# Where source order begins, two sums and a sign on GpSimd, and values one slot earlier, in a single-core attention and feed-forward kernel

## The chip, the cores and the metric

The kernel runs on one core of a Trainium2 chip. A core has TensorE (PE, matmuls, with its weight loads shown as PEld), VectorE (DVE), ScalarE (ACT), GpSimd (POOL) and a queue that issues DMAs (SP). Each engine works through its own instructions in a fixed order and waits on semaphores for the others. The metric is the device time of one execution in microseconds. Three runs of the kernel before gave 858.89, 858.98 and 859.55 us, a median of 858.98. The profile is of one further execution, which took 860.12 us; its span from the first to the last instruction is 858.2 us.

## The reference

Attention in chunks of 64 tokens, without any link between chunks, then a feed-forward layer with a gate:

```python
scores = scale * np.matmul(q_c, k_c.transpose(0, 1, 2, 4, 3))
scores = scores - np.max(scores, axis=-1, keepdims=True)
attn = np.exp(scores)
attn = attn / (np.sum(attn, axis=-1, keepdims=True) + 1e-09)
out = np.matmul(attn, v_c)
...
h = x @ w_in
relu6 = np.clip(h + 3.0, 0.0, 6.0)
g = h * relu6 / 6.0
return (g @ w_out).astype(np.float32)
```

q, k and v have the shape (8, 8, 576, 64) in float32. x has 4608 tokens of 512 values, w_in is 512 x 2048 and w_out 2048 x 512. The reference makes the weights in float64, and the kernel gets them as pairs of 32-bit words.

## The kernel before

The 4608 tokens are nine blocks of 512. Every product of the feed-forward layer is made of three TensorE passes (`passes`, lines 219 to 223): each float32 operand is split into a high part and a low part in TensorE's format fp32r, and high x high, high x low and low x high are summed. So for each operand there is a copy that rounds (on ScalarE) and a subtraction that gives the rest (on VectorE).

The first three blocks take the plain way, and this case is about them. The 2048 hidden values are 16 f tiles of 128. For one f tile of one block, `mm1` (225) makes h with 12 matmuls of 512 columns, L233 and L234 apply the gate, L235 rounds g and L236 subtracts for g's low half. `mm2` (242) adds the f tile to the four accumulators (`acc`, `ps_o`) with 12 more matmuls. It runs two f tiles behind `mm1` (`LAG` = 2). The blocks come in four segments: block 0 f tiles 0 to 3, block 1 all 16, block 0 f tiles 4 to 15, block 2 all 16 (line 29). Block 0's first four f tiles are put away as `part` and added when its second segment ends (L259). The last six blocks go through a scheme with fewer multiplications (lines 471 to 630), which needs sums and differences of quarters of the weights in DRAM.

A slot is one `mm1` or one `mm2`. Slots are counted over the four segments: block 1 begins with slot 8, so its f tile k has the slots 8 + 2k and 9 + 2k; there are 96. `plan` holds side work for each slot, run after the slot's matmuls are written (line 443). `finish` (215) then writes the subtractions that were put into `low`, L236 among them.

Three kinds of side work matter here:

- Conversions (`convert`, 100 to 116). A weight tile of 128 x 1024 float64 values arrives as words; ScalarE scales the high word (L106), VectorE shifts the result by three bits (L107) and puts the sign bit of the high word on it (L108), adds the low word that ScalarE scaled (L110, L111), and the result is split (L115, L116). There are 16 tiles. The scratch pool `wsc` holds u and r twice each, at the right end of SBUF. The first four tiles are converted in the opening and block 0's first segment, the other twelve in block 1.
- Attention (`Attention`, 128 to 209), a piece of a block at a time: scores (64 small matmuls into two PSUM banks, `ps_a`), softmax in four steps on VectorE and ScalarE, eight transposes into the same two banks, a copy back to SBUF on ScalarE (L185), values (64 small matmuls into the same banks), a copy out (L200, or L203 with L206). `ps_a` has one buffer, so each step waits until the one before it has left the banks. The list `later` (401) puts the steps of six attentions at slots relative to 30, 38, 52, 60, 68 and 76.
- Sums of the weights (`prepare`, 325 to 353), sixteen of them in three steps each: three DMAs of w and two sums of the low and high part (L334), then four sums and differences (L344) and a rounding copy to `hl` (L347), then a subtraction (L349) and four DMAs of hl. `a` and `hl` have one buffer each. They lie in the pool `sp`, which is opened where `wsc` was.

Up to slot `SUMS` the order on each engine is made by the language's planner, from its own costs; `issue_after` holds VectorE's conversions of tiles 4 and later behind block 1's attention. At slot `SUMS` (20, block 1's f tile 6) the scratch pool is closed, `sp` and `op` are opened, and `manual_schedule` sets source order for everything that follows (436 to 441). The sums are spread from `SUMS` to two slots before `FREE` (86), a start every four slots.

Of the kernel before, what the change touches and what calls it, by code (L numbers as in the profile page):

```python
# [8 lines left out]
F32 = mybir.dt.float32  # L9
F32R = mybir.dt.float32r  # L10
BF16 = mybir.dt.bfloat16
I32 = mybir.dt.int32
U32 = mybir.dt.uint32
AF = mybir.ActivationFunctionType
ALU = mybir.AluOpType
AX = mybir.AxisListType

P = 128
# [7 lines left out]
NCT, NFT, NET = DM // P, DFF // P, DO // P  # L26
# [15 lines left out]
def tile_kernel(ctx: ExitStack, tc: tile.TileContext, qk_in, v_in, weights, out):  # L42
    nc = tc.nc
    PE, ACT, DVE, POOL = nc.tensor, nc.scalar, nc.vector, nc.gpsimd
# [17 lines left out]
    op = None  # L62
# [29 lines left out]
    def load_to(ft):  # L92
        nonlocal loaded
        while loaded < min(ft, NFT):
            t = w_tile(loaded, I32).rearrange("p l m t -> p (l m t)")
            nc.sync.dma_start(out=t.rearrange("p (m t) -> p m t", m=2), in_=weights[loaded].bitcast(I32).rearrange("m p t -> p m t"))
            words[loaded] = t.rearrange("p (n t) -> p n t", t=2)
            loaded += 1

    def convert(ft):  # L100

        u = wsc.tile([P, 1024], I32, name="u")
        r = wsc.tile([P, 1024], I32, name="r")
        lo, hi = words[ft][:, :, 0], words[ft][:, :, 1]

        ACT.activation(out=u.bitcast(F32), in_=hi.bitcast(F32), func=AF.Copy, scale=2.0 ** -112)  # L106
        DVE.tensor_scalar(out=u, in0=u, scalar1=3, scalar2=None, op0=ALU.logical_shift_left)  # L107
        DVE.scalar_tensor_tensor(out=u, in0=hi, scalar=-2 ** 31, in1=u, op0=ALU.bitwise_and, op1=ALU.bitwise_or)  # L108

        ACT.activation(out=r, in_=lo.bitcast(U32), func=AF.Copy, scale=2.0 ** -29)  # L110
        DVE.tensor_tensor(out=u, in0=u, in1=r, op=ALU.add)  # L111
        a = u.bitcast(F32).rearrange("p (m t) -> p m t", m=2)
        w[ft] = w_tile(ft, F32R)
        w_h[ft], w_l[ft] = w[ft][:, 0], w[ft][:, 1]
        ACT.copy(out=w_h[ft], in_=a)  # L115
        DVE.tensor_tensor(out=w_l[ft], in0=a, in1=w_h[ft].bitcast(F32), op=ALU.subtract)  # L116

    def convert_to(ft):
        nonlocal converted
        load_to(ft + 3)  # L120
        while converted < min(ft, NFT):
            convert(converted)
            converted += 1
# [91 lines left out]
    def finish():  # L215
        while low:
            low.pop(0)()

    def passes(ps, a_h, a_l, b_h, b_l, first, last, more=False):

        PE.matmul(ps, lhsT=a_h, rhs=b_h, start=first, stop=False, skip_group_check=more)  # L221
        PE.matmul(ps, lhsT=a_h, rhs=b_l, start=False, stop=False, skip_group_check=more)  # L222
        PE.matmul(ps, lhsT=a_l, rhs=b_h, start=False, stop=last, skip_group_check=more)  # L223
# [15 lines left out]
    acc = []  # L239
    part = {}  # L240

    def mm2(n, ft, g, first, last, spill):

        if first:
            acc[:] = [ps_o.tile([P, NT], F32, name="acc") for et in range(NET)]
        for et in range(NET):
            o = slice(et * P, (et + 1) * P)
            passes(acc[et], w_h[ft][:, 1, o], w_l[ft][:, 1, o], g[:, 0, :], g[:, 1, :], first, last)
            if last:
                before = part.get((n, et))  # L250
                if spill:
                    t = keep.tile([P, NT], F32, name=f"part{n}_{et}")
                elif op:
                    t = op.tile([P, NT], F32, name="o")
                else:
                    o2 = o2 if et % 2 else gp.tile([P, 2, NT], F32, name="g")
                    t = o2[:, et % 2]
                if before is not None:
                    DVE.tensor_tensor(out=t, in0=acc[et], in1=before, op=ALU.add)  # L259
                elif et % 2:  # L260
                    DVE.tensor_copy(out=t, in_=acc[et])
                else:
                    ACT.copy(out=t, in_=acc[et])
                if spill:
                    part[n, et] = t
                else:
                    nc.sync.dma_start(out=out[o, n * NT:(n + 1) * NT], in_=t)
# [16 lines left out]
    keep = rpool("keep", 1)  # L284
    scratch = ExitStack()
    wsc = scratch.enter_context(tc.tile_pool(name="wsc", bufs=2, side="right"))

    with tc.tile_pool(name="ps_b", bufs=2, space=bass.MemoryType.PSUM) as ps_b:
        both = [Attention(0, dp, lambda: two_banks(ps_b)) for dp in range(NDP)]
# [35 lines left out]
    def prepare(m, p):  # L325
        cols = lambda k: slice(256 * k, 256 * k + 256)
        for i, row, col in ((1, 0, 0), (2, 0, 1), (4, 1, 1)):
            f, k = quarter(m, row, col)
            to = kept(m, p, i).rearrange("p (l t) -> p l t", l=2)
            nc.sync.dma_start(out=to, in_=w[p + NFP * f][:, :, m, cols(k)].bitcast(F32))  # L330
        a = sp.tile([P, 2, 512], F32, name="a")
        for f in range(2):
            h, l = [w[p + NFP * f][:, k, m].bitcast(F32) for k in range(2)]
            DVE.tensor_tensor(out=a[:, f], in0=h, in1=l, op=ALU.add)  # L334
        yield

        def q(row, col):
            f, k = quarter(m, row, col)
            return a[:, f, cols(k)]


        for to, x, y, op in ((q(1, 1), q(1, 0), q(1, 1), ALU.add), (q(1, 0), q(0, 0), q(1, 0), ALU.subtract),
                             (q(0, 0), q(1, 1), q(0, 0), ALU.subtract), (q(0, 1), q(0, 1), q(0, 0), ALU.subtract)):
            DVE.tensor_tensor(out=to, in0=x, in1=y, op=op)  # L344
        hl = sp.tile([P, 2, 2, 2, 256], F32R, name="hl")
        s = a.rearrange("p f (k t) -> p f k t", k=2)
        ACT.copy(out=hl[:, :, :, 0], in_=s)  # L347
        yield
        DVE.tensor_tensor(out=hl[:, :, :, 1], in0=s, in1=hl[:, :, :, 0].bitcast(F32), op=ALU.subtract)  # L349
        for i, row, col in ((5, 1, 1), (7, 1, 0), (6, 0, 0), (3, 0, 1)):  # L350
            f, k = quarter(m, row, col)
            nc.sync.dma_start(out=kept(m, p, i), in_=hl[:, f, k].rearrange("p l t -> p (l t)").bitcast(F32))
        yield
# [23 lines left out]
    def x_operands(s, eng):  # L377
# [6 lines left out]
        for i in ORDER_A:  # L384
# [6 lines left out]
            elif i == 6:  # L391
# [7 lines left out]
    plan = {}  # L399
    early = [(0, "load_qk"), (1, "load_v"), (2, "scores"), (2, "softmax"), (7, "transpose"), (10, "values")]  # L400
    later = [(-2, "load_qk"), (3, "load_v"), (3, "scores"), (4, "soft", 0), (4, "soft", 1), (5, "soft", 2), (5, "soft", 3),
             (8, "transpose"), (10, "values")]

    def put(n, dp, at, steps, stretch=1.0):
        a = Attention(n, dp)
# [4 lines left out]
    put(1, 0, -2, early, 0.45)  # L410
    second = put(1, 1, 3, early, 0.45)
    first = [2 * sum(hi - lo for _, lo, hi in SEGMENTS[:i]) for i in range(len(SEGMENTS) + 1)]
    SUMS = first[1] + 12
    FREE = first[3] + 2 * (NFP + LAG + 1)
    for (n, dp), at in zip(((2, 0), (2, 1), (3, 0), (4, 0), (4, 1), (3, 1)), (30, 38, 52, 60, 68, 76)):
        put(n, dp, at, later)
    for u in range(2 * NFP):
        for k in range(3):
            plan.setdefault(SUMS + u * (FREE - 2 - SUMS) // (2 * NFP) + k, []).append((20, lambda: next(prep)))
    prep = (step for p in range(NFP) for m in range(2) for step in prepare(m, p))  # L420
# [4 lines left out]
    for i, (n, lo, hi) in enumerate(SEGMENTS):  # L425
        last = all(m != n for m, *_ in SEGMENTS[i + 1:])
        for ft in range(lo, hi):
            if i == 0:
                convert_to(min(ft + 2, 4))
            elif slot < SUMS:  # L430

                with tc.issue_after(second.done.ins):
                    convert_to(5)
                with tc.issue_after(second.last.ins):
                    convert_to(6 + 2 * ft)
            elif slot == SUMS:
                scratch.close()
                sums = ExitStack()
                sp = sums.enter_context(tc.tile_pool(name="sp", bufs=1, side="right"))
                op = sums.enter_context(tc.tile_pool(name="op", bufs=4, side="right"))  # L440
                order.enter_context(tc.manual_schedule())
            for _ in moe_slots(n, ft, ft == lo, ft == hi - 1, not last):
                for _, f in sorted(plan.pop(slot, []), key=lambda s: s[0]):
                    f()
                finish()
                slot += 1
                if slot == FREE:
                    assert next(prep, None) is None
                    sums.close()
                    op = None  # L450
                    start.close()
                    upper.close()
                    xop_pool = pool("xop", 8, side="right")
                    wsp = pool("wsp", 3, side="right")
                    for _ in range(3):
                        fetch()
                    made = x_operands(0, DVE)
                elif slot > FREE:
                    next(made, None)

    for item in pending:
        mm2(*item)
# [4 lines left out]
    op = pool("op2", 2)  # L467
# [189 lines left out]
```

## Time and profile before

| what | value |
|---|---|
| median of three runs | 858.98 us |
| the profiled execution | 860.12 us |
| its span | 858.2 us |
| mean granted TensorE clock | 0.974 |
| TensorE busy with matmuls | 813.4 us (95%) |
| VectorE busy | 636.2 us (74%) |
| ScalarE busy | 367.4 us (43%) |
| GpSimd busy | 128.9 us (15%) |

TensorE is busy in nearly all of the span, so time is lost where it stands idle or runs at a lower clock. The page shows the span in 40 equal slices of 21.5 us; the digits are the busy share in tenths:

```profile
PE   6988929999998999999999999999999999999998
PEld 4766818878876878878878888788788887887886
DVE  6978996776767667487699956876999466669951
ACT  4747744244243335334356442344554433336330
POOL 0000000000000000021318003212270022335200
PEclk9798969999998999999999999999999999999999
```

PE's line has a 2 in the sixth slice (107 to 129 us), where the clock also falls to 0.6, while DVE's line has a 9 there. The thirteenth slice (257 to 279 us) has an 8. The first two slices are the opening: loads, the first attention, the first conversions. GpSimd does next to nothing before the eighteenth slice.

A row of the timeline has the start, the duration, the engine, the line, the operation, the written and read names with their shapes, and in brackets the idle time of the engine before it with what ended that. A row of the list of waits has the waiting instruction, what it waited for, the total, the number of times and the longest.

### The profile page before, as it was taken

What the parts mean: (1) busy time and instruction counts of PE and PEld (TensorE: products, weight loads), DVE (VectorE), ACT (ScalarE), POOL (GpSimd) and SP (SyncE); (2) the same over time, 40 slices, a digit from 0 to 9 for tenths busy, and PEclk for the clock granted to TensorE, in tenths of its full rate; (3) what the DMA queues carried; (4) which work ended last, traced back from release to release, by engine and by line L of the source; (5) the groups of instructions that cost most, each with busy time, mean ns of one, the idle gap of its engine ahead of it and who ended that gap; (6) DMA issues with size and microseconds to landing.
All of it is one profiled execution on the core that took longest, in us unless ns stands there. A gap on an engine that the chain in (4) does not pass through costs nothing.

```text
span 858.2 us, 13692 instructions
## 1 busy us (share of the span) xinstructions
PE 813.4 (95%) x5683; PEld 659.2 (77%) x5683; DVE 636.2 (74%) x770; ACT 367.4 (43%) x453; POOL 128.9 (15%) x75
## 2 busy tenths in 40 slices
PE   6988929999998999999999999999999999999998
PEld 4766818878876878878878888788788887887886
DVE  6978996776767667487699956876999466669951
ACT  4747744244243335334356442344554433336330
POOL 0000000000000000021318003212270022335200
PEclk9798969999998999999999999999999999999999
DMA  9791006767664565156555676666555765555564
GB/s 365 298 375 67 13 0 215 218 203 249 208 207 174 175 231 210 49 222 238 204 191 215 244 224 232 227 238 224 199 194 183 223 228 187 193 200 196 196 208 136
DMA packets 50014, 172.86 MB, mean 201 GB/s; under 512 B 4640, under 2 KB 16928, under 8 KB 39200
## 3 DMA queue, kind: packets, MB, share of 16 engines
q1 hardware_dynamic: 49952, 171.99, 57.6%
q8 instruction: 45, 0.74, 0.3%
q14 instruction: 17, 0.14, 0.0%
HBM read 133.17 MB, written 38.80 MB: 200 GB/s over the span
## 4 chain that ended last, share of the span: by engine, by line
PE 64%; DVE 21%; ACT 6%; issue 4%; DMA 3%; SPq 1%; POOL 0%; ACTq 0%; DVEq 0%
PE acc L221 14%; PE acc L222 13%; PE acc L223 13%; PE h L221 6%; PE h L222 6%; PE h L223 6%; DVE xop L370 2%; PE two L194 2%; DVE a L344 2%; ACT r L233 2%; DVE r L234 1%; DMA w<-w_in_out 1%; DVE z L168 1%; DVE m L161 1%; PE two L154 1%
## 5 line engine op out<-in xcount | busy, mean ns | idle before, releaser
L221 PE MATMUL acc<-xop,ws 128*128 128x512 f32 x528 | 208.8, 396 | 4.4 <-DVE u L481 4.4
L222 PE MATMUL acc<-xop,ws 128*128 128x512 f32 x528 | 206.0, 390 | 0.0
L223 PE MATMUL acc<-xop,ws 128*128 128x512 f32 x528 | 205.6, 390 | 0.0
L501 POOL TENSOR_TENSOR g<-g 128x512 f32<-128x512 f32 x24 | 34.8, 1448 | 572.0 <-DVE g L493 572.0
L221 PEld LDWEIGHTS acc<-xop,ws 128*128 128x128 f32 x528 | 99.2, 188 | 27.7 <-DVE u L481 6.8
L370 DVE TENSOR_TENSOR xop<-g,xop 128x1024 fp32r<-128x1024 f32 x72 | 103.3, 1466 | 21.5 <-ACT xop L369 21.5
L223 PEld LDWEIGHTS acc<-xop,ws 128*128 128x128 f32 x528 | 99.2, 188 | 20.9
L222 PEld LDWEIGHTS acc<-xop,ws 128*128 128x128 f32 x528 | 99.3, 188 | 19.6
L369 ACT CAST xop<-g 128x1024 fp32r<-128x1024 f32 x72 | 74.4, 1050 | 78.9 <-PE acc L223 51.3
L222 PE MATMUL acc<-g,w 128*128 128x512 f32 x192 | 77.3, 403 | 16.4 <-DVE g L236 16.4
L221 PE MATMUL acc<-g,w 128*128 128x512 f32 x192 | 77.6, 408 | 3.3 <-DVE o L259 3.3
L221 PE MATMUL h<-x,w 128*128 128x512 f32 x192 | 78.3, 410 | 2.3 <-ACT x L203 1.9
L234 DVE SCALAR_TENSOR_TENSOR r<-r,h 128x512 f32<-128x512 f32 x48 | 32.8, 684 | 62.6 <-ACT r L233 62.5
L222 PE MATMUL h<-x,w 128*128 128x512 f32 x192 | 77.6, 405 | 0.0
L223 PE MATMUL acc<-g,w 128*128 128x512 f32 x192 | 77.2, 402 | 0.0
L223 PE MATMUL h<-x,w 128*128 128x512 f32 x192 | 76.9, 401 | 0.0
L492 ACT ACTIVATE r<-acc,half 128x512 f32<-128x512 f32 x72 | 48.5, 685 | 26.3 <-DVE acc L481 25.4
L492 ACT ACTIVATE r<-h,half 128x512 f32<-128x512 f32 x24 | 16.5, 687 | 94.9 <-DVE h L481 94.9
L222 PE MATMUL h<-xop,ws 128*128 128x512 f32 x144 | 56.2, 391 | 0.2 <-DVE xop L370 0.2
L222 PEld LDWEIGHTS acc<-g,w 128*128 128x128 f32 x192 | 37.1, 193 | 25.0 <-DVE g L236 17.2
L221 PE MATMUL h<-xop,ws 128*128 128x512 f32 x144 | 56.4, 391 | 0.0
L223 PE MATMUL h<-xop,ws 128*128 128x512 f32 x144 | 56.2, 390 | 0.0
(91 smaller groups left out, 1275.4 us busy)
## 6 DMA issues: line engine op xcount, KB each, us to landing
ws<-b SPq DMA_DIRECT2D x42, 1024.0 KB, 4.8
ws<-a SPq DMA_DIRECT2D x24, 1024.0 KB, 4.8
ws<-a SPq DMA_DIRECT2D x24, 768.0 KB, 4.3
qk<-qk_in SPq DMA_DIRECT2D x17, 1024.0 KB, 6.5
w<-w_in_out SPq DMA_DIRECT2D x16, 1024.0 KB, 13.2
v<-v_in SPq DMA_DIRECT2D x17, 512.0 KB, 5.4
a<-hl SPq DMA_DIRECT2D x32, 256.0 KB, 3.4
b<-hl SPq DMA_DIRECT2D x32, 256.0 KB, 3.0
```

What stands on the lines that cost most here:

```text
L154: PE.matmul(self.s[o, a, c, :], lhsT=self.qk[rows, 0, c, o], rhs=self.qk[rows, 1, c, o], start=True, stop=True)
L194: PE.matmul(po[o, s, a, i, :], lhsT=self.v[rows, a, i, o], rhs=self.aT[rows, a, i, o], start=True, stop=True)
L221: PE.matmul(ps, lhsT=a_h, rhs=b_h, start=first, stop=False, skip_group_check=more)
L222: PE.matmul(ps, lhsT=a_h, rhs=b_l, start=False, stop=False, skip_group_check=more)
L223: PE.matmul(ps, lhsT=a_l, rhs=b_h, start=False, stop=last, skip_group_check=more)
L233: ACT.activation(out=r, in_=h, func=AF.Relu, bias=half, scale=1.0 / 6.0)
L234: DVE.scalar_tensor_tensor(out=r, in0=r, scalar=1.0, in1=h, op0=ALU.min, op1=ALU.mult)
L344: DVE.tensor_tensor(out=to, in0=x, in1=y, op=op)
L369: ACT.copy(out=t[:, :, 0], in_=src)
L370: DVE.tensor_tensor(out=t[:, :, 1], in0=src, in1=t[:, :, 0].bitcast(F32), op=ALU.subtract)
L492: return (lambda: ACT.activation(out=r, in_=ps, func=AF.Relu, bias=half, scale=1.0 / 6.0), lambda: DVE.scalar_tensor_tensor(out=out, in0=r ...
L501: sub = lambda o, x, y: lambda: POOL.tensor_tensor(out=o, in0=x, in1=y, op=ALU.subtract)
```

## The change

Four things change.

1. `SUMS` goes from `first[1] + 12` (slot 20, f tile 6 of block 1) to `first[1] + 22` (slot 30, f tile 11). The planner makes the order of ten slots more, the scratch pool is closed ten slots later, and the sixteen sums start every three or four slots from slot 30 to slot 80. `min(6 + 2 * ft, NFT)` keeps the number of tiles asked for at 16.
2. In block 0's final sums (four parts, `et` 0 to 3) the odd two are made by a copy on ScalarE and an addition in SBUF on GpSimd, where VectorE made them from PSUM.
3. In `later`, values stand one slot behind the transposes, where they stood two behind.
4. In a conversion, GpSimd multiplies the high word, read as a float32, by zero, which leaves a zero with the word's sign. VectorE then shifts by three and joins the sign in one instruction, where it had two. The sign tile has its own pool with one buffer.

```diff
@@ -104,8 +104,10 @@
         ACT.activation(out=u.bitcast(F32), in_=hi.bitcast(F32), func=AF.Copy, scale=2.0 ** -112)
-        DVE.tensor_scalar(out=u, in0=u, scalar1=3, scalar2=None, op0=ALU.logical_shift_left)
-        DVE.scalar_tensor_tensor(out=u, in0=hi, scalar=-2 ** 31, in1=u, op0=ALU.bitwise_and, op1=ALU.bitwise_or)
+
+        sign = sgn.tile([P, 1024], F32, name="sign")
+        POOL.tensor_scalar(out=sign, in0=hi.bitcast(F32), scalar1=0.0, scalar2=None, op0=ALU.mult)
+        DVE.scalar_tensor_tensor(out=u, in0=u, scalar=3, in1=sign.bitcast(I32), op0=ALU.logical_shift_left, op1=ALU.bitwise_or)
@@ -255,7 +257,10 @@
-                if before is not None:
+                if before is not None and et % 2:
+                    ACT.copy(out=t, in_=acc[et])
+                    POOL.tensor_tensor(out=t, in0=t, in1=before, op=ALU.add)
+                elif before is not None:
                     DVE.tensor_tensor(out=t, in0=acc[et], in1=before, op=ALU.add)
@@ -284,6 +289,7 @@
     wsc = scratch.enter_context(tc.tile_pool(name="wsc", bufs=2, side="right"))
+    sgn = scratch.enter_context(tc.tile_pool(name="sgn", bufs=1, side="right"))
@@ -399,7 +405,7 @@
     later = [(-2, "load_qk"), (3, "load_v"), (3, "scores"), (4, "soft", 0), (4, "soft", 1), (5, "soft", 2), (5, "soft", 3),
-             (8, "transpose"), (10, "values")]
+             (8, "transpose"), (9, "values")]
@@ -410,7 +416,7 @@
-    SUMS = first[1] + 12
+    SUMS = first[1] + 22
@@ -432,7 +438,7 @@
                 with tc.issue_after(second.last.ins):
-                    convert_to(6 + 2 * ft)
+                    convert_to(min(6 + 2 * ft, NFT))
```

## The prediction

> **What bounds the kernel now.** I read the busy time by stretches first, then the list of waits, then the timeline of VectorE and TensorE around the longest wait.
>
> ```profile
> 72.00:107.00 35.00, 34.57 (x147) 27.33 (x146) 34.17 (x39) 27.86 (x33) 0.00 (x0) 0.99 0.02 8
> 107.00:127.00 20.00, 3.58 (x17) 2.61 (x15) 18.33 (x20) 10.21 (x11) 0.00 (x0) 0.66 0.00 0
> 127.00:330.00 203.00, 196.49 (x1560) 159.09 (x1560) 139.44 (x219) 74.40 (x100) 0.00 (x0) 0.97 0.64 204
> ...
> PE acc L222 <- DVE g L236: 16.4, 1, 16.4
> ...
> PE acc L221 <- DVE o L259: 3.3, 1, 3.3
> ...
> PE two L194 <- ACT e L185: 2.9, 3, 1.2
> ...
> PE two L154 <- ACT x L200: 2.4, 2, 1.5
> ```
>
> The columns of the first three rows are the stretch, its length, then busy time (and instructions) of PE, weight loads, DVE, ACT and POOL, the granted clock, the DMA share and GB/s. TensorE sets the time nearly everywhere: 34.57 of 35 us and 196.49 of 203 us busy. The exception is the 20 us between them, where it works 3.58 us and VectorE 18.33. That hole is one wait of 16.4 us, for the low half of g that L236 writes. Three small waits follow: for accumulators to be emptied (L259, 3.3 us) and for the two banks that attention reuses (L200, 2.4 us in two waits).
>
> ```profile
> 106.03 1.23 DVE L116 TENSOR_TENSOR w<-u,w 128x1024 fp32r<-128x1024 f32 x1
> ...
> 123.71 1.23 DVE L116 TENSOR_TENSOR w<-u,w 128x1024 fp32r<-128x1024 f32 x1 [1.17 <-ACT w L115]
> 124.97 1.29 DVE L334 TENSOR_TENSOR a<-w 128x512 f32<-128x512 f32 x2
> 126.18 0.68 DVE L236 TENSOR_TENSOR g<-r,g 128x512 fp32r<-128x512 f32 x1
> ...
> 110.11 0.39 PE L221 MATMUL acc<-g,w 128*128 128x512 f32 x1
> 126.92 0.79 PE L222 MATMUL acc<-g,w 128*128 128x512 f32 x1 [16.42 <-DVE g L236]
> ...
> 130.49 0.43 PE L221 MATMUL acc<-g,w 128*128 128x512 f32 x1
> ```
>
> The columns are start, duration and instruction. L334 is the first of the weights' sums. It writes a tile that lies where the conversions' scratch lay, so it cannot start before the sixteenth conversion ends (L116 at 123.71 plus 1.23). From slot 20 on the order is that of the source, so L236 of block 1's seventh f tile stands behind it. The twelfth conversion was at its last step at 106.03, so four were still open when TensorE arrived. The eight matmul starts from 126.92 to 130.49 stand 0.446 us apart (in the first stretch 34.57 us held 147 matmuls, 0.235 each), so the low clock after the hole costs another 1.7 us. The hole is worth 16.4 + 1.7 = 18.1 us.
>
> **The change, part by part.** (1) *Source order from slot 30.* The slots between go back to the planner, ten slots of 12 matmuls, 28 us. One conversion ran per f tile:
>
> ```profile
> 83.51 0.69 DVE L107 TENSOR_SCALAR u<-u 128x1024 int32<-128x1024 int32 x1
> 84.11 0.68 DVE L234 SCALAR_TENSOR_TENSOR r<-r,h 128x512 f32<-128x512 f32 x1
> 84.72 1.23 DVE L116 TENSOR_TENSOR w<-u,w 128x1024 fp32r<-128x1024 f32 x1
> 85.86 1.22 DVE L108 SCALAR_TENSOR_TENSOR u<-w,u 128x1024 int32<-128x1024 int32 x1
> 87.00 0.69 DVE L236 TENSOR_TENSOR g<-r,g 128x512 fp32r<-128x512 f32 x1
> 87.60 1.22 DVE L111 CUSTOM_DVE_ANT_0 u<-u,r 128x2048 uint16<-128x2048 uint16 x1
> 88.74 0.69 DVE L107 TENSOR_SCALAR u<-u 128x1024 int32<-128x1024 int32 x1
> ```
>
> A round takes 88.74 - 83.51 = 5.23 us on VectorE, against 24 x 0.235 = 5.6 us on TensorE. At 5.6 us a round the last four conversions end near 106.0 + 1.2 + 4 x 5.6 = 129.6. L236 of the twelfth f tile, now the first behind L334, is then done at 129.6 + 1.2 + 0.7 = 131.5. TensorE needs it five f tiles after the present hole, at 110.1 + 28 + 0.2 = 138.3. The margin is 6.8 us, so the whole 18.1 us goes, and nothing is late next at that place.
>
> The sixteen sums are the same work, squeezed from 64 slots into 54. VectorE was busy 139.44 of 203 us there; in 28 us less it is 80% busy, still covered by TensorE. A sum now follows the last after 3 or 4 slots instead of 4, and its L347 must wait until the DMAs of the last one have read hl. Such a wait (4.89 us before 147.19, first row below) did not stop TensorE, which was busy 10.00 of those 10 us; its cover is the two f tiles between a gate and its use. Each sum issues seven DMAs on SP's queue, three of w and four of hl. The DMA share goes from 0.64 to some 0.64 x 203 / 175 = 0.74. The loads of q, k and v between them keep their slots, five or more ahead of their use (14 us), so I cost their delay at nothing; POOL's queue is empty there.
>
> ```profile
> 147.19 1.05 ACT L347 CAST hl<-a 128x1024 fp32r<-128x1024 f32 x1 [4.89 <-DMA b<-hl]
> ...
> 140.00:150.00 10.00, 10.00 (x46) 8.29 (x45) 6.21 (x12) 3.23 (x5) 0.00 (x0) 1.00 0.90 272
> ...
> 168.01 0.38 PE L183 MATMUL two<-ident,e 128*128 128x128 f32 x2
> ...
> 174.12 1.01 ACT L185 COPY e<-two 128x1024 f32<-128x1024 f32 x1
> ...
> 238.84 0.62 ACT L235 CAST g<-r 128x512 fp32r<-128x512 f32 x1 [0.76 <-DVE r L234]
> ...
> 241.17 0.62 ACT L235 CAST g<-r 128x512 fp32r<-128x512 f32 x1 [1.12 <-DVE r L234]
> 241.70 1.01 ACT L185 COPY e<-two 128x1024 f32<-128x1024 f32 x1
> ...
> L183 PE MATMUL two<-ident,e x8: 271/272/273, 322.4 to 323.2; 128*128 128x128 f32 x8
> ...
> 327.18 1.01 ACT L185 COPY e<-two 128x1024 f32<-128x1024 f32 x1
> ```
>
> (2) *Values one slot after transposes* instead of two, in six attentions. This adds a wait. Values read what L185 copies, and L185 stands on ScalarE behind L235 of its slot. L235 waits for L234, and L234 waits on VectorE behind sums and softmax (238.84 to 241.70 above). So L185 ends late: 174.12 + 1.01 is 6.1 us after the first attention's eight transposes end (168.01 + 1.04, their time in the next fence). For the six it is 6.1, 5.5, 4.9, 7.1, 4.6 and 4.7 us, the last from 323.5 to 328.2. Before, 24 matmuls (5.6 us) lay between; now 12 do, 2.8 us. What is left over is 3.3 + 2.7 + 2.1 + 4.3 + 1.8 + 1.9 = 16.1 us of TensorE waiting, with all later matmuls queued behind. The first gets some 2 us more (its L347 is one that would stand two slots behind the last sum, with hl still being read); the fourth some 2 less, since it lies behind the L259 rows that (3) thins. They cancel. Before, 0.6 us of this was already there, so 15.5 us is new. In return, values leave the banks a slot sooner, and the two waits for L200 go: 2.4 us.
>
> ```profile
> L263 ACT COPY o<-acc x2: 567/578/589, 188.5 to 189.0; 128x512 f32<-128x512 f32 x2
> ...
> 248.78 1.16 PE L154 MATMUL two<-qk 64*64 64x64 f32 x64 [1.45 <-ACT x L200]
> ...
> 263.81 1.04 PE L183 MATMUL two<-ident,e 128*128 128x128 f32 x8
> 267.32 2.48 DVE L259 TENSOR_TENSOR o<-acc,part 128x512 f32<-128x512 f32 x4
> 268.15 0.77 PE L221 MATMUL acc<-g,w 128*128 128x512 f32 x1 [3.30 <-DVE o L259]
> ...
> 273.83 0.44 PE L222 MATMUL h<-x,w 128*128 128x512 f32 x1
> ```
>
> (3) *Two of block 0's four sums on GpSimd.* ScalarE copies two accumulators (0.58 us each, by the first row) beside two adds on VectorE, and L349, which stood just ahead, falls in another slot. The first accumulator is free some 2.2 us earlier: 3.3 us becomes 1.1. Thirteen matmul steps from 268.15 to 273.83 took 0.437 us instead of 0.235, 2.6 us; after 1.1 us of waiting I expect none of that, since matmuls after the 1.45 us wait for L200 came at full pace. Worth 2.2 + 2.6 = 4.8 us. The GpSimd adds feed only output DMAs.
>
> (4) *Sign on GpSimd.* L107 goes, 0.60 us of each conversion; the new combined step takes L108's place and 1.14 us. VectorE's round falls to 4.63 us. GpSimd gets one instruction of 128x1024 elements, one input, which the trace does not have. Its neighbours:
>
> ```profile
> L381 POOL TENSOR_TENSOR x<-x x8: 2394/2403/2417, 453.8 to 691.6; 128x1024 f32<-128x1024 f32 x8
> ...
> L65 POOL MEMSET r<- x1: 524/524/524, 0.7 to 0.7; 128x512 f32 x1
> ...
> L550 POOL TENSOR_TENSOR g<-g,t x12: 3315/3382/3397, 458.5 to 795.4; 128x1024 f32<-128x1024 f32 x12
> ...
> L548 DVE TENSOR_TENSOR g<-t,g x12: 1208/1218/3429, 386.9 to 793.1; 128x1024 f32<-128x1024 f32 x12
> ```
>
> L548, two SBUF inputs, takes 1.21 us alone and 3.43 beside L550: GpSimd's work is added to VectorE's. So a GpSimd product of length H costs VectorE up to H a round. Twice the memset is 1.05 us, the two-input L381 2.40 us. I take 1.05, the row with one stream. The round is then 5.68 us, 0.08 over TensorE's 5.6; by the source twelve of the sixteen conversions lie in block 1, so 1 us. The ends are 0 (no collision: the round of 4.63 hides under TensorE, which was already full, so nothing is gained) and 12 x (4.63 + 2.40 - 5.6) = 17.2 us. The other four stand in the opening, where one conversion more or less on VectorE can move the first products: between 4 x -0.60 and 4 x (2.40 - 0.60), -2.4 to +7.2 us. I take 0, because the 1.05 and the 0.60 nearly balance and not all of it lies on the path.
>
> A slow clock after the new waits: the first, some 5 us, gets the 2.6 us seen after 3.3 us; the others lie between 1.45 (none) and 3.3 us, and I take 1 us for all.
>
> By the Trainium skill ("TensorE: Matmul & The Clock Gate", Part 1) the clock halves after an idle window of about 3.4 us. Here 3.30 us was enough. By the page alone that 1 us would be 0, and the sum 1 us better.
>
> **The sum.** Gains 18.1 + 4.8 + 2.4 = 25.3; losses 15.5 + 2.6 + 1 + 1 = 20.1; net -5.2 us. The profiled execution took 860.1 us (span 858.2), 1.1 above the median of 858.98. Both ends of my sum lie inside the span, so I subtract from the median: **853.8 us**.
>
> **Rivals.** *A, the forecast:* hole gone, values late; 848 to 857.3 with the sizes of the waits, clock and copies. *B, values are not late:* if less softmax and sum work stands ahead of L185 in the new order, it ends within 2.8 us, and between a third and most of the 19.1 us that A loses to late values falls away (6 to 17 us): 837 to 848. For it: the sums' steps fall in other slots than before. Against: even the best of the six was 4.6 us, of which L233, L234, L235 and L185 in a row need 2.9. *C, GpSimd blocks VectorE:* at H = 2.40 the conversions cost 12 x 1.35 = 16.2 us more than in A, L334 again starts late and TensorE waits at the new boundary: 853.8 + 16.2 = 870.0, slower than before. It decides from H = 1.05 + 5.2/12 = 1.5 us. For it: L548 beside L550. Against: one input, not two.
>
> The Trainium skill ("SBUF — State Buffer", SBUF: two separate sides) says that a VectorE instruction with two SBUF inputs and a GpSimd instruction exclude each other for the whole instruction. The 3.43 us of L548 agrees; it speaks for C. "GPSIMD Engine Reference", Engine selection, calls one-input work roughly line-rate, which speaks for A's 1.05; no run here shows it yet.
>
> That the hole stays because the planner again leaves conversions to the boundary is part of C: the same wait, the same signs.
>
> **Chances.** A 0.57, B 0.24, C 0.19. A's own range is 848 to 857. With the low half of B below 842 (0.1) and the upper part of C above 862 (0.1) left out, the range is 842 to 862. The bound of 0.2% is 1.7 us, about what a measurement can tell from no change. Faster: B and nearly all of A, 0.78; same: A's edge and C's lower part, 0.09; slower: 0.13.
>
> **What would show it.** Right: no wait of TensorE for L236 over 1 us near the new boundary; six waits of values for L185 of 2 to 5 us; L200 gone from the waits; the accumulators' wait near 1 us; GpSimd's product near 1.05 us. Wrong: L185's waits below 1 us in total (B), or VectorE's combined step and L111 well over 1.3 us beside a product over 1.5 us, with TensorE idle between 67 and 140 (C).

## The result, and the profile after

| what | before | after |
|---|---|---|
| median, us (4 runs of each on one chip) | 859.26 (858.89 to 860.04) | 879.28 (878.73 to 880.67) |
| span of the profiled execution, us | 858.2 | 877.3 |
| mean granted TensorE clock | 0.974 | 0.973 |

The ratio is 1.0241, with a 95% interval of 1.0219 to 1.0263: the kernel is slower, by 20 us. The forecast was 853.8 with a range of 842 to 862, so both its sign and its range were wrong. One execution on record, the profiled one of experiment 9, ran at a granted clock of 0.556 and took 1341.08 us; no figure here includes it.

To find the place, take the starts of the same f tiles in both timelines. The first fence is before, the second after; each row is the first matmul of an f tile's `mm1`: f tiles 1, 2, 8 and 12 of block 1 and f tile 11 of block 2. The diff adds lines, so a number of before stands two further in after from L108 on in `convert` and in most of what follows (L185 becomes L187, L194 L196, L234 L236, L236 L238), and six further in the weights' sums (L347 becomes L353). `passes` (L219 to L223) becomes L221 to L225.

```profile
67.42 0.79 PE L221 MATMUL h<-x,w 128*128 128x512 f32 x1 [1.87 <-ACT x L203]
...
72.85 0.39 PE L221 MATMUL h<-x,w 128*128 128x512 f32 x1
...
107.36 0.39 PE L221 MATMUL h<-x,w 128*128 128x512 f32 x1
...
147.64 0.39 PE L221 MATMUL h<-x,w 128*128 128x512 f32 x1
...
326.05 0.39 PE L221 MATMUL h<-x,w 128*128 128x512 f32 x1
```

```profile
72.86 0.50 PE L223 MATMUL h<-x,w 128*128 128x512 f32 x1 [2.90 <-ACT x L205]
...
77.94 0.56 PE L223 MATMUL h<-x,w 128*128 128x512 f32 x1
...
132.41 0.39 PE L223 MATMUL h<-x,w 128*128 128x512 f32 x1
...
154.35 0.39 PE L223 MATMUL h<-x,w 128*128 128x512 f32 x1
...
346.20 0.50 PE L223 MATMUL h<-x,w 128*128 128x512 f32 x1
```

| stretch | before, us | after, us | difference | forecast for it |
|---|---|---|---|---|
| opening, to f tile 1 | 67.42 | 72.86 | +5.4 | 0 |
| f tile 1 to 2 | 5.43 | 5.08 | -0.4 | 0 |
| f tile 2 to 8 | 34.51 | 54.47 | +20.0 | +1 |
| f tile 8 to 12, with the hole | 40.28 | 21.94 | -18.3 | -18.1 |
| f tile 12 to block 2's f tile 11 | 178.41 | 191.85 | +13.4 | +11.9 |

The last forecast is 15.5 + 2.6 + 1 - 2.4 - 4.8, the terms of late values, slow clock, L200 and accumulators. Two rows came out near the forecast, the last of them in part by luck (see the section on why). The opening and the six f tiles ahead of the hole did not: together they cost 25.4 us, and 1 us was forecast.

These are TensorE's rows in the list of waits of after (what waits, for what, us in all, times, the longest):

```profile
PE two L196 <- ACT e L187: 16.4, 6, 5.6
...
PE h L223 <- DVE r L236: 10.7, 5, 2.8
PE h L223 <- ACT x L205: 5.5, 2, 2.9
PE h L224 <- DVE x L208: 4.7, 2, 4.2
...
PE acc L224 <- DVE g L238: 1.8, 1, 1.8
```

The wait for the low half of g is down from 16.4 us to 1.8, and that one ends at 83.11, far ahead of the new boundary. The two waits for L200 and that for the emptied accumulators are gone. The six waits of values are there, 16.4 us against a forecast of 16.1. What is new is that `mm1` waits for the gate's first step, L236: it reads the h of an earlier f tile, and until it has, the buffer cannot be written. The busy times by stretches show where (columns as before):

```profile
73.00:91.00 18.00, 15.32 (x55) 11.08 (x56) 15.82 (x15) 12.24 (x14) 10.73 (x4) 0.91 0.29 110
91.00:127.00 36.00, 25.48 (x85) 19.05 (x84) 35.37 (x29) 26.22 (x29) 26.11 (x7) 0.85 0.02 8
127.00:154.00 27.00, 27.00 (x114) 22.04 (x114) 11.56 (x17) 8.06 (x12) 0.00 (x0) 0.95 0.00 1
```

From 91 to 127 VectorE is busy 35.37 of 36 us and TensorE 25.48, at a granted clock of 0.85. In the next 27 us VectorE is busy 11.56. So VectorE's work was not spread over the ten slots that the planner had been given: it was piled up in front, and then there was little left to do. Of the 20.0 us lost in the six f tiles, 12.5 are the waits for L236 and L238. Some 6 us more are the low clock: behind each of the four longest of these waits nine matmul steps take 3.6 us (from 95.31 to 98.96, for one), where nine of 0.235 would be 2.1. The timeline of all engines shows the pile:

```profile
95.69 1.22 DVE L118 TENSOR_TENSOR w<-u,w 128x1024 fp32r<-128x1024 f32 x1
95.85 3.77 POOL L109 TENSOR_SCALAR sign<-w 128x1024 f32<-128x1024 f32 x1 [1.35 <-DVE u L110]
96.82 2.16 DVE L113 CUSTOM_DVE_ANT_0 u<-u,r 128x2048 uint16<-128x2048 uint16 x1
...
98.90 0.68 DVE L238 TENSOR_TENSOR g<-r,g 128x512 fp32r<-128x512 f32 x1
...
99.66 1.23 DVE L110 SCALAR_TENSOR_TENSOR u<-u,sign 128x1024 int32<-128x1024 int32 x1
100.80 1.22 DVE L118 TENSOR_TENSOR w<-u,w 128x1024 fp32r<-128x1024 f32 x1
101.94 2.14 DVE L113 CUSTOM_DVE_ANT_0 u<-u,r 128x2048 uint16<-128x2048 uint16 x1
...
104.00 0.68 DVE L236 SCALAR_TENSOR_TENSOR r<-r,h 128x512 f32<-128x512 f32 x1
...
104.73 0.50 PE L223 MATMUL h<-x,w 128*128 128x512 f32 x1 [2.81 <-DVE r L236]
```

Read VectorE's rows in order: the three steps of one conversion, L238, the three steps of another, L236. An f tile needs one L236 and one L238, so each f tile now carries *two* conversions, where before it carried one (the round from 83.51 to 88.74 in the prediction). A conversion takes 100.80 - 95.69 = 5.11 us, two take 10.2, and TensorE has 5.6 us of work per f tile. The ring is closed on GpSimd as well: the product ends at 95.85 + 3.77 = 99.62, L110 starts at 99.66, and the next product waits until L110 has read the only sign tile (the 1.35 us in its row). VectorE itself hardly stands still for the sign here: it is idle for 0.63 of these 36 us.

In the opening it is the product's length that is late:

```profile
32.31 3.90 POOL L109 TENSOR_SCALAR sign<-w 128x1024 f32<-128x1024 f32 x1 [6.53 <-DVE u L110]
...
36.25 1.23 DVE L110 SCALAR_TENSOR_TENSOR u<-u,sign 128x1024 int32<-128x1024 int32 x1 [2.76 <-POOL sign L109]
37.39 1.22 DVE L208 TENSOR_TENSOR x<-two,x 128x1024 fp32r<-128x1024 f32 x1
...
38.66 0.79 PE L224 MATMUL h<-x,w 128*128 128x512 f32 x1 [4.16 <-DVE x L208]
```

VectorE stands 2.76 us at L110 for the sign. L208, which gives attention's result to `mm1`, is queued behind it, and TensorE waits 4.16 us for L208. The instruction itself, in the view by source line (least, median and longest ns of its 16):

```profile
L109 POOL TENSOR_SCALAR sign<-w x16: 2822/3744/3905, 14.6 to 121.4; 128x1024 f32<-128x1024 f32 x16
```

### The profile page after: what moved, and what is told of

Its sections match the earlier page's. It is cut to its first block, busy times and chain, and to the rows that moved or that the text cites. A ratio compares the mean times of both kernels' runs of the same rounds, so it can differ in the third digit from the quotient of the medians.

```text
span 877.3 us, 13733 instructions
## 1 busy us (share of the span) xinstructions
PE 823.9 (94%) x5683; PEld 664.3 (76%) x5683; DVE 638.5 (73%) x752; ACT 370.1 (42%) x455; POOL 186.9 (21%) x93
## 4 chain that ended last, share of the span: by engine, by line
PE 60%; DVE 17%; issue 9%; POOL 6%; ACT 4%; DMA 3%; SPq 1%; ACTq 0%; DVEq 0%; POOLq 0%
PE acc L223 13%; PE acc L225 13%; PE acc L224 13%; PE h L223 6%; PE h L224 6%; PE h L225 6%; POOL sign L109 6%; DVE xop L376 2%; PE two L196 2%; DMA w<-w_in_out 1%; DVE z L170 1%; DVE m L163 1%; DVE a L350 1%; DVE r L236 1%; DVE g L499 1%
## 5 line engine op out<-in xcount | busy, mean ns | idle before, releaser
L223 PE MATMUL acc<-xop,ws 128*128 128x512 f32 x528 | 208.7, 396 | 4.4 <-DVE u L487 4.4
L225 PE MATMUL acc<-xop,ws 128*128 128x512 f32 x528 | 205.4, 390 | 0.0
L223 PEld LDWEIGHTS acc<-xop,ws 128*128 128x128 f32 x528 | 99.1, 188 | 27.7 <-DVE u L487 6.8
L225 PEld LDWEIGHTS acc<-xop,ws 128*128 128x128 f32 x528 | 99.2, 188 | 21.0
L223 PE MATMUL h<-x,w 128*128 128x512 f32 x192 | 83.0, 434 | 17.9 <-DVE r L236 10.7
L224 PE MATMUL h<-x,w 128*128 128x512 f32 x192 | 82.2, 429 | 4.7 <-DVE x L208 4.7
L225 PE MATMUL h<-x,w 128*128 128x512 f32 x192 | 80.3, 419 | 0.0
L236 DVE SCALAR_TENSOR_TENSOR r<-r,h 128x512 f32<-128x512 f32 x48 | 32.8, 684 | 64.4 <-ACT r L235 64.4
L224 PE MATMUL acc<-g,w 128*128 128x512 f32 x192 | 75.7, 394 | 1.9 <-DVE g L238 1.8
L225 PE MATMUL acc<-g,w 128*128 128x512 f32 x192 | 75.5, 393 | 0.0
L223 PE MATMUL acc<-g,w 128*128 128x512 f32 x192 | 74.1, 396 | 0.1
L109 POOL TENSOR_SCALAR sign<-w 128x1024 f32<-128x1024 f32 x16 | 54.9, 3433 | 68.5 <-DVE u L110 55.7
L223 PEld LDWEIGHTS h<-x,w 128*128 128x128 f32 x192 | 38.9, 203 | 30.2 <-DVE r L236 13.1
L224 PE MATMUL h<-xop,ws 128*128 128x512 f32 x144 | 56.2, 390 | 0.1
L223 PE MATMUL h<-xop,ws 128*128 128x512 f32 x144 | 56.3, 391 | 0.0
## 6 DMA issues: line engine op xcount, KB each, us to landing
w<-w_in_out SPq DMA_DIRECT2D x16, 1024.0 KB, 11.6
```

What stands on the lines that cost most here:

```text
L109: POOL.tensor_scalar(out=sign, in0=hi.bitcast(F32), scalar1=0.0, scalar2=None, op0=ALU.mult)
L236: DVE.scalar_tensor_tensor(out=r, in0=r, scalar=1.0, in1=h, op0=ALU.min, op1=ALU.mult)
```

## The experiments

The theory at this point: the loss is made by the sign product, through the order (two conversions beside one f tile) and through its length of 2.8 to 3.9 us; the other edits did what the forecast said. The rivals: the product's length alone, or its collision with VectorE alone (rival C); or the late values costing more than their waits.

**1 and 2. One part of the change undone.** In the first, the two old instructions on VectorE come back in the changed kernel:

```diff
-        sign = sgn.tile([P, 1024], F32, name="sign")
-        POOL.tensor_scalar(out=sign, in0=hi.bitcast(F32), scalar1=0.0, scalar2=None, op0=ALU.mult)
-        DVE.scalar_tensor_tensor(out=u, in0=u, scalar=3, in1=sign.bitcast(I32), op0=ALU.logical_shift_left, op1=ALU.bitwise_or)
+        DVE.tensor_scalar(out=u, in0=u, scalar1=3, scalar2=None, op0=ALU.logical_shift_left)
+        DVE.scalar_tensor_tensor(out=u, in0=hi, scalar=-2 ** 31, in1=u, op0=ALU.bitwise_and, op1=ALU.bitwise_or)
```

> The changed kernel with the conversion as it was before (part 4 undone, no sign product on GpSimd). Theory 1, the sign product costs the loss: the opening's 5 us and the 20 us between block 1's third and ninth f tile go, no wait comes back where source order begins, the six waits for L185 (16 us) stay: 854 us, between 850 and 858. Theory 2, the planner's ten extra slots cost the loss and the product little: over 868 us.

Measured: 855.64 us (854.68 to 856.26), 0.9952 of before (0.9937 to 0.9967). These are the first matmuls of block 1's f tiles 2 and 8 in its timeline:

```profile
72.03 0.50 PE L221 MATMUL h<-x,w 128*128 128x512 f32 x1
...
106.44 0.39 PE L221 MATMUL h<-x,w 128*128 128x512 f32 x1
```

The opening is that of before (f tile 1 starts at 66.77), the six f tiles take 34.4 us again, and VectorE has one conversion per f tile. The hole stays away, since the last four conversions run beside the f tiles after the eighth. So the sign product costs 879.28 - 855.64 = 23.6 us here, and the other three edits together bring 3.9 us (859.58 for the kernel before beside it), where the forecast has 6.2 for them: its 5.2 and the 1 us that it charges to the sign.

In the second, values go back to slot 10:

```diff
-             (8, "transpose"), (9, "values")]
+             (8, "transpose"), (10, "values")]
```

> The changed kernel with values two slots after transposes, as before (part 3 undone). If the six waits for L185 cost what they show (16.4 us and some 3 us of slow clock behind them) and the waits for L200 that come back cost 2 to 6 us: 866 us, between 862 and 870. If the waits are free because something else is late then: 877 to 880.

Measured: 866.97 us (866.63 to 867.41), 12.3 less than after. Its list of waits has 4.3 us for L187 in place of 16.4, and two waits for L202 (L200 of before) are back with 3.4 us. The late values cost 12.3 us with the sign product still there, so independently of it. Their waits have the forecast's size; their net price is less than the forecast's terms for it (the section on why has the sum).

**3. The same product, one conversion per f tile.** The number of tiles asked for at each f tile grows by one in place of two, so that the order holds the conversions apart:

```diff
-                    convert_to(min(6 + 2 * ft, NFT))
+                    convert_to(min(6 + ft, NFT))
```

> The changed kernel, but block 1 asks for one conversion per f tile, not two. The product stays as long, 3.75 us. Theory 1a, the loss is the order times the loop over the single sign buffer (two rounds of 5.1 us in one f tile of TensorE's 5.6): one round of 5.1 us fits under 5.6, so TensorE no longer waits for L236's line there and the 17 to 20 us go, the opening's 5 us stay: 860 us, between 857 and 864. Theory 1b, the product's length or its collision with VectorE costs the time whatever the order: over 872 us.

Measured: 862.64 us (861.01 to 863.4), 1.0032 of before (1.0019 to 1.0045). Its timeline:

```profile
73.11 0.50 PE L223 MATMUL h<-x,w 128*128 128x512 f32 x1 [2.91 <-ACT x L205]
...
78.12 0.63 PE L223 MATMUL h<-x,w 128*128 128x512 f32 x1
...
97.19 1.22 DVE L118 TENSOR_TENSOR w<-u,w 128x1024 fp32r<-128x1024 f32 x1
97.36 3.76 POOL L109 TENSOR_SCALAR sign<-w 128x1024 f32<-128x1024 f32 x1 [1.77 <-DVE u L110]
98.33 1.60 DVE L238 TENSOR_TENSOR g<-r,g 128x512 fp32r<-128x512 f32 x1
99.85 1.21 DVE L113 CUSTOM_DVE_ANT_0 u<-u,r 128x2048 uint16<-128x2048 uint16 x1
...
114.03 0.39 PE L223 MATMUL h<-x,w 128*128 128x512 f32 x1
```

The product is as long as in the changed kernel (3.76 us) and still lengthens a VectorE instruction, now L238 (1.60 for 0.68). Yet the six f tiles take 114.03 - 78.12 = 35.9 us, 1.4 more than before. So with one conversion per f tile the long product costs 1.4 us there: the forecast's 1 us was right for the order that it assumed. The opening's loss stays (73.11).

**4. The same order, a short product.** The product makes the signs of 256 columns, and the combined step uses them four times; the signs of the other three quarters are left out.

```diff
-        POOL.tensor_scalar(out=sign, in0=hi.bitcast(F32), scalar1=0.0, scalar2=None, op0=ALU.mult)
-        DVE.scalar_tensor_tensor(out=u, in0=u, scalar=3, in1=sign.bitcast(I32), op0=ALU.logical_shift_left, op1=ALU.bitwise_or)
+        POOL.tensor_scalar(out=sign[:, :256], in0=hi[:, :256].bitcast(F32), scalar1=0.0, scalar2=None, op0=ALU.mult)
+        v = u.rearrange("p (a t) -> p a t", a=4)
+        DVE.scalar_tensor_tensor(out=v, in0=v, scalar=3, in1=sign[:, :256].bitcast(I32).unsqueeze(1).broadcast_to([P, 4, 256]), op0=ALU.logical_shift_left, op1=ALU.bitwise_or)
```

> The changed kernel with the sign product on a quarter of the columns, read four times by VectorE (the sign of three quarters of the weights is left out); VectorE's order is the same instruction by instruction. Theory 1a, the pace was set by product plus combined step, 3.75 + 1.35 us a round: now VectorE's own work sets it, two conversions of 3.4 us and 1.3 us of gates in one f tile, 8.1 us instead of 10.2, so TensorE still waits some 2.5 us in each of five f tiles: 864 us, between 861 and 869, the opening's loss mostly gone. Theory 1c, only the product's length counts and the order is harmless: 854 us, as with the sign back on VectorE. Theory 1d, only the order counts: 875 to 880 us.

Measured: 864.53 us (864.16 to 865.87), 1.006 of before (1.0045 to 1.0075). Its timeline (a line more, so L113 is L114 here and L236 is L237):

```profile
66.31 0.50 PE L224 MATMUL h<-x,w 128*128 128x512 f32 x1 [2.36 <-ACT x L206]
...
71.58 0.50 PE L224 MATMUL h<-x,w 128*128 128x512 f32 x1
...
90.49 1.77 POOL L109 TENSOR_SCALAR sign<-w 128x256 f32<-128x256 f32 x1 [2.45 <-DVE u L111]
91.46 1.43 DVE L114 CUSTOM_DVE_ANT_0 u<-u,r 128x2048 uint16<-128x2048 uint16 x1
...
93.54 0.50 PE L224 MATMUL h<-x,w 128*128 128x512 f32 x1 [2.08 <-DVE r L237]
...
117.68 0.39 PE L224 MATMUL h<-x,w 128*128 128x512 f32 x1
```

The opening's loss is gone (66.31), so that loss is the product's length. But the six f tiles take 117.68 - 71.58 = 46.1 us, with GpSimd idle 2.45 us before each of the last five products. Of their 20.0 us, 46.1 - 34.5 = 11.6 stay with a short product, which still takes 0.21 us of VectorE's time in a conversion (1.43 for 1.22): that is the order, nearly by itself. The other 8.4 come with the full length of the product within that order.

**5. The sign and the values back.** Source order from slot 30 and the two sums on GpSimd are kept: experiments 1 and 2 at once.

> Parts 3 and 4 undone: what is left of the change is source order from slot 30 and the two sums on GpSimd. If the parts add up as the runs so far say (sign back 855.6, values later worth 12.3 us): 843 us, between 839 and 846, faster than both kernels. If they only hide one another (the waits for L185 fill with other waits once nothing holds TensorE earlier): 850 us or more.

Measured: 844.76 us (842.29 to 845.92), 0.9824 of before (0.9807 to 0.9841). This is faster than both kernels, and near the 843 of parts that add up.

**6 and 8. One part alone, on the kernel before.** The edit of 6 is the values' line of the change, that of 8 its sign product with the pool.

> The kernel before with part 3 alone, values one slot after transposes. Theory, L185 ends late whatever the rest: five or six waits of 1 to 4 us for L185 appear, the two for L200 go, 870 us, between 866 and 875. Rival, the waits of the changed kernel came from the sums being closer together: within 2 us of before.

> The kernel before with part 4 alone, the sign product on GpSimd and source order from slot 20. The planner puts two conversions beside one f tile as in the changed kernel, and the hole at slot 20 takes up most of what that costs, since it waits for the same last conversion: that ends some 3 us later than before, so 863 us, between 860 and 868. If the product's costs add to the hole instead: 880 us or more.

Measured: 870.7 us (869.29 to 874.02), 1.0135 (1.0111 to 1.0159), for the values; 866.19 us (865.21 to 866.31), 1.0077 (1.0061 to 1.0094), for the sign product. Neither edit pays by itself. With the values alone, five of the six attentions wait for L185, 1.8 to 2.8 us each and 11.5 in all, and the waits for L200 are gone; so the late copy does not need the new place of the sums. The kernel with the sign alone is only 7 us slower although its order ahead of the boundary is that of after (waits of 2.8 us for L236, and 73.78 us to f tile 1), because the hole has gone into it: from f tile 8 to 12 it takes 21.9 us, as after. The last conversion ends at 131.97, 7.0 us later than before (124.94), and f tile 12 starts 7.6 later. Delay ahead of the boundary and hole at the boundary are the same work of VectorE, paid once. In the changed kernel, moving the boundary had removed the hole already, and the delay is paid in full.

**7. Is the step of the input the reason for the length?** The high words lie two words apart. Here the product reads u, which lies without a gap; it is the scaled high word and has its sign.

```diff
-        POOL.tensor_scalar(out=sign, in0=hi.bitcast(F32), scalar1=0.0, scalar2=None, op0=ALU.mult)
+        POOL.tensor_scalar(out=sign, in0=u.bitcast(F32), scalar1=0.0, scalar2=None, op0=ALU.mult)
```

> The changed kernel, but the sign product reads ScalarE's scaled copy of the high word (which has the same sign and lies without gaps), not the high word in steps of eight bytes. If the step makes the product slow, its shortest time falls from 2.82 us to under 1.9 us. If the instruction has that rate itself: 2.7 to 2.9 us. The planner makes another order for it, so its total time tells nothing of the length.

Measured (one profiled run, 870.75 us), in the view by source line:

```profile
L109 POOL TENSOR_SCALAR sign<-u x16: 2772/3106/3841, 15.7 to 131.1; 128x1024 f32<-128x1024 f32 x16
```

The shortest is 2.77 us against 2.82. The step isn't the cause; this instruction has this rate. The time itself isn't compared: with u as its input the product stands behind L106, which changes the order too.

**9 and 10. Around the faster version.** From the kernel of experiment 5, the ninth moves the six attentions one slot forward:

```diff
-             (8, "transpose"), (10, "values")]
+             (7, "transpose"), (9, "values")]
```

> The change with its sign product undone, and with the six attentions' transposes at slot 7 and their values at slot 9 (two slots apart as before the change, but one slot earlier both). Theory (what lies between the transposes and the values is all that counts; the banks come free a slot sooner): the waits for L200 go as in the changed kernel, and values stay in time as in the run with transposes at 8 and values at 10: 842 us (840 to 844), some 2 to 3 us under that run. Rival (softmax is not ready a slot sooner, so the transposes wait for it on TensorE): new waits of transposes for L172, 845 to 850 us.

Measured: 843.78 us, the median of three (841.4 to 844.21), ratio 0.9815 (0.9788 to 0.9842). That is 1.0 us under experiment 5, with intervals that overlap: no gain can be told, and no clear loss as the rival has it. The waits of these three were not profiled.

The tenth takes the two sums of block 0 back to VectorE:

```diff
-                if before is not None and et % 2:
-                    ACT.copy(out=t, in_=acc[et])
-                    POOL.tensor_tensor(out=t, in0=t, in1=before, op=ALU.add)
-                elif before is not None:
+                if before is not None:
                     DVE.tensor_tensor(out=t, in0=acc[et], in1=before, op=ALU.add)
```

> Only the source order from slot 30; the two sums of block 0 stay on VectorE, the values at slot 10 and the sign on VectorE. The prediction's term for the two sums on GpSimd is 4.8 us (2.2 of waiting and 2.6 of slow clock). If that term is right, this run is 4.8 us slower than the one with the sums on GpSimd: 849 to 850 us, with a wait for L259 of some 3 us near the end of block 0. Rival (the wait went because the order of the weights' sums changed, not because of GpSimd): 844 to 846 us with a wait near 1 us or none.

Measured: 845.5 us (841.17 to 847.33), 0.9837 (0.9796 to 0.9878), so 0.7 us over experiment 5, with overlapping intervals again. Its list of waits:

```profile
PE acc L221 <- DVE o L259: 1.0, 1, 1.0
```

The wait for L259 is 1.0 us without any sum on GpSimd. So most of what the prediction gave to the two sums came with the later start of source order: 2.3 of the 3.3 us of waiting. What is left for the sums to remove is this 1.0 us; the totals scatter by more than that, so their own worth can't be told.

## Why the prediction was wrong, point by point

- **The hole (18.1 us).** Right: -18.3 us from f tile 8 to 12 with TensorE busy all of 127 to 154, and no wait for the low half of g at the new boundary. In experiment 1, without the pile ahead of it, this stretch takes 23.0 us, 17.3 less than before.
- **Values late (six waits, 16.1 us).** Right in mechanism, place and size of the waits: 16.4 us in six, the longest 5.6. The chain was the one named: L187 behind L353, L235 and L237 on ScalarE. In the timeline of after, with the transposes first:

```profile
174.72 1.03 PE L185 MATMUL two<-ident,e 128*128 128x128 f32 x8
...
180.12 1.04 ACT L353 CAST hl<-a 128x1024 fp32r<-128x1024 f32 x1 [4.65 <-DMA b<-hl]
...
182.51 0.62 ACT L237 CAST g<-r 128x512 fp32r<-128x512 f32 x1 [0.76 <-DVE r L236]
183.04 1.00 ACT L187 COPY e<-two 128x1024 f32<-128x1024 f32 x1
```

  The copy ends 8.3 us after the transposes (184.04 against 175.75), 2.2 later than for the first attention before, because L353 waits for hl's DMAs: the "some 2 us more" of the prediction. Rival B fell. The net price was too high, though: 15.5 + 2.6 + 1 - 2.4 = 16.7 us by the prediction's terms, but 12.3 in experiment 2, 11.2 in experiment 6 and 10.9 between experiments 5 and 1. In the new order some waiting is there with values at slot 10 too: in experiment 5 the six attentions wait some 3.9 us for L185 (0.6 before) and 3.7 for L200 (2.4 before).
- **Accumulators (4.8 us).** The wait went, but the step gave it to the wrong edit. "The first accumulator is free some 2.2 us earlier" was reckoned with the order of before; experiment 10 shows the wait at 1.0 us in the new order with all four sums on VectorE. Nor did the 4.8 us come out as time: with values at slot 10, in experiment 5, f tile 12 to block 2's f tile 11 takes 178.7 us, 0.3 more than before, as the waits just named grew. So in this stretch the forecast's -4.8 and +16.7 stand against measured +0.3 and +13.1, and that +13.4 came out near +11.9 is luck in part.
- **The sign product. Here the prediction failed**, in two steps. The first: "The round is then 5.68 us, 0.08 over TensorE's 5.6", which set one round against one f tile. The round came out shorter, 5.11 us, but two of them stood beside each f tile. The fence that showed one conversion per f tile showed an order that the planner had made for the old instructions; the text carried it over to new ones. Experiment 3 shows that the order decides (1.4 us with the same product, one per f tile), experiment 4 that it costs 11.6 of the 20.0 us even with a short product. The prediction had the new planner leave conversions to the boundary as its only fault of order; the fault was the opposite one, conversions taken too early. Why the planner packs two together stays open: the runs show its order, not the costs that it goes by.
- The second step: "I take 0, because the 1.05 and the 0.60 nearly balance", for the opening. It priced what the product takes from VectorE, and not what it adds to the conversion's chain: VectorE stands in its queue (2.76 us at 36.25) for a result that takes 2.8 to 3.9 us, with L208 behind it. Experiment 4, with the short product, has the opening of before again. The opening's +5.4 us lay within the bound given there (+7.2), but not in the range handed down, since the value taken was 0.
- **The size of the product.** Neighbours gave 1.05 and 2.40 us, the last meant as the upper end. It takes 2.82 alone: a one-input operation was slower than the two-input addition. What VectorE *loses* to it, 2.16 - 1.22 = 0.94 us, came out near the 1.05 by luck: the length was taken 2.7 times too short, and a loss of the whole length was assumed where a third of it was lost.
- **Rival C** named the right edit, the right stretch (67 to 140) and the right sign, and its 870.0 was nearer than the forecast. Its mechanism, VectorE blocked for the length of the product, isn't what happened; nor did L334 start late at the boundary (as L340 of after it starts at 153.22, when VectorE has long been free). Of its signs, a product over 1.5 us, L111 well over 1.3 (2.16, as L113 of after) and an idle TensorE were seen; the combined step stayed at 1.23.

Up to f tile 8 the measured loss is 132.41 - 107.36 = 25.0 us, where the forecast has 1. With it the prediction's own sum gives 853.8 + 24.0 = 877.8, beside 879.28 measured. By experiment 1 the sign product costs 23.6 us where 1 was forecast, which is 22.6 of the miss of 25.5. That the rest fits so closely rests in part on the two misses that cancel in the last stretch.

## What to carry to other kernels

An instruction moved to another engine has two prices: what it takes there from its neighbours, and how long its result is away from the engine that stands waiting for it in order. Both were paid here: 0.94 us in most conversions of the pile, where VectorE hardly stood still, and in the opening 2.76 us of standing, for which TensorE waited 4.16. Whether a second sign buffer would help was not tested. Where a planner makes the order, an order read from the profile holds for the instructions it was made for, so an edit of the planned instructions needs a price for the order turning out denser or looser. And test the edits of a bundle one by one: here source order from slot 30 brings nearly all of the gain (845.5 alone), and two of its three companions more than give it back.

## What the hardware showed that was not expected

- GpSimd's product with a constant takes 2.82 us for 128 x 1024 float32 values and 0.86 for 128 x 256 (the shortest of experiment 4), more than its two-input addition of 128 x 1024 (2.40 in the prediction's rows).
- Beside VectorE the product takes 3.77 us, 0.95 more than alone, and the VectorE instruction that follows its start takes 0.94 more. In the timeline of after, L118 started 0.16 us ahead of the product and was not lengthened; the product seems to stand until L118 ends, and L113, which starts then, is late by 0.94 us and not by the 2.7 that the product still needs. With 256 columns the losses are 0.91 for the product (1.77 against 0.86) and 0.21 for L114. The spans on GpSimd are rough in these profiles; the 0.94 and the 0.21 are VectorE's own. The Trainium skill ("SBUF — State Buffer", SBUF: two separate sides) has whichever of the two starts first, a VectorE instruction with two SBUF inputs or a GpSimd one that reads SBUF, hold the shared ports for its whole instruction. That agrees with the product standing behind L118, and with L548 beside a two-input addition (3.43 for 1.21). It disagrees with L113, which lost a third of the product's length.
- Idle stretches of 2.1 to 2.8 us, one in every 10 us, were enough for a granted clock of 0.85 from 91 to 127. The prediction took 3.30 us as the shortest wait with a slow clock behind it, but the 1.87 us at 67.42 before (the first fence of the result) has one too, with waits of 2.00 and 1.10 us in the 7 us ahead of it: 0.79 us in that row, 0.39 in the next. The length of a wait alone does not settle it: behind 1.72 us at 315.88 after, eight matmul steps stand 0.42 apart, and behind 2.69 us at 288.26 none does.
